# One full-size product in place of the turn and the spread in a kernel's scale chain

## The chip, the core and the metric

The kernel runs on one core of one Trainium2 chip. The core has five engines that work through queues of their own and wait for one another by semaphores: TensorE (PE in the profile, its weight loads PEld), VectorE (DVE), ScalarE (ACT), GpSimd (POOL) and SyncE (SP, which here only issues transfers). The metric is the device time of one execution in microseconds (us); lower is better.

## What is computed

Three stages follow one another, all of them in single precision at the interface: attention with a window of 128 and a distance bias on 4 x 8 heads of 576 positions; a mixture of eight experts over the 2304 tokens that come out, whose weights are normalised by eight rounds over rows and columns; and a feed-forward layer of width 2048 with a leaky maximum.

```python
def _attn_ref(q, k, v):                     # q, k, v: 4 x 8 x 576 x 64
    scores = scale * np.matmul(q, k.transpose(0, 1, 3, 2))
    mask = (rel >= 0) & (rel < 128)
    scores = np.where(mask, scores + bias[None], -1000000000.0)
    attn = np.exp(scores - np.max(scores, axis=-1, keepdims=True))
    attn = attn / (np.sum(attn, axis=-1, keepdims=True) + 1e-09)
    return np.matmul(attn, v)

def _moe_ref(x, w_gate, w1, w2):            # x: 2304 x 512, eight experts of 512 x 1024 x 512
    P = np.exp(x @ w_gate - (x @ w_gate).max())
    for _ in range(8):
        P /= P.sum(1, keepdims=True) + 1e-09
        P /= P.sum(0, keepdims=True) + 1e-09
        P *= N / E
    for e in range(E):
        out += P[:, e:e + 1] * (np.maximum(x @ w1[e], 0.0) @ w2[e])
    return out

def _moe2_ref(x, w_in, w_out):              # 512 x 2048 x 512
    h = x @ w_in
    return np.maximum(0.01 * h, h) @ w_out
```

## The kernel before

**Products.** Every large product is made of float16 matmuls. An operand is split into a high and a low float16 part (`split`), three of the four part products are kept, and a 2 x 2 block product is made with seven products in place of eight (`PRODUCTS`). For float16 to be exact enough, each operand is first multiplied by a power of two that brings its largest entry to a fixed place; the power is taken out again when the result is scaled. The float16 matmuls have 128 rows and 128 columns of weights and mostly 256 columns of moving data; they stand on lines 774 (first layer, results `s` and `sq`) and 891 (second layer, result `t`).

**The scale chain.** `scale_jobs` works out such a power for one operand. It is called 51 times: five times for the attention output of a token group (`Inputs`, phase 0), once for the gate weights, forty times for a chunk of weights (`Weights`, twice for each of the 20 chunks, with `squares=True`) and five times for the input of the last layer (`Inputs`, phase 1). It returns jobs, one a tick, with `None` for ticks that are left out:

- `one` (L453 to L459): VectorE reduces the per-partition values `mx` to one column `m` and keeps the exponent bits of it, `e`.
- `two` (L461 to L478): the column is turned into a row: a matmul with `e`, read as bfloat16, as one column of weights and the bfloat16 identity as 128 columns of moving data gives `mt`, one row of 128. VectorE reduces that row to one number `k` and makes the power and its reciprocal of it, `b`, all on one partition.
- `three` (L480 to L483): the two numbers are spread to all partitions: a matmul with a row of ones, `onesb`, as weights of one row and `b` as two columns of moving data gives `st`, 128 x 2. VectorE copies it to `sr`, from which `scaled` (L625), `turned`, `weigh` and `back` read.

Both results lie in a PSUM bank that `small_psum` gives out: after the attention stage from the same pair of banks that the results `t0` of the second layer use in turn; during it from the one bank `s1`.

**The order.** The work is put into queues (`side`, `inputs`, `gating`, `fill`) from which `tick` takes a job after each step of seven matmul groups or so. The tile framework then orders each engine's instructions by a timeline that it works out itself (`schedule_with_timeline_sim=True`), so that a change of one job can move others, in the attention stage above all, where PE, DVE and ACT have much to choose from. PE, DVE, ACT and POOL take their instructions strictly in the order that results.

**The stages in the trace**, in us from the start: attention, the first weight chunk and the token groups up to about 212; the rounds of the gate beside products up to about 300; the experts up to about 1470; the change from the experts to the last layer, where the inputs are turned, scaled and split again, up to about 1620; the rest of the last layer up to 1904.

Of the kernel before, what the change touches and what calls it, by code (L numbers as in the profile page):

```python
# [8 lines left out]
F32 = mybir.dt.float32  # L9
F16 = mybir.dt.float16  # L10
BF16 = mybir.dt.bfloat16
I32 = mybir.dt.int32
U32 = mybir.dt.uint32
AF = mybir.ActivationFunctionType
ALU = mybir.AluOpType
# [16 lines left out]
def attn_moe_kernel(  # L32
# [12 lines left out]
    nc = tc.nc  # L45
    P = 128
# [23 lines left out]
    const = ctx.enter_context(tc.tile_pool(name="const", bufs=1))  # L70
# [5 lines left out]
    small = ctx.enter_context(tc.tile_pool(name="small", bufs=2))  # L76
# [5 lines left out]
    identb = const.tile([P, P], BF16, name="identb")  # L82
# [3 lines left out]
    ones = const.tile([P, P], F32, name="ones")  # L86
    nc.vector.memset(ones, 1.0)
    shift = const.tile([P, 1], F32, name="shift")
    nc.vector.memset(shift, float(-(896 << 23)))
    onesb = const.tile([1, P], BF16, name="onesb")  # L90
    nc.vector.memset(onesb, 1.0)
    wg = const.tile([P, KT, E], F32, name="wg")
    qscale = const.tile([P, NP], F32, name="qscale")
    Pm = const.tile([P, NTILE, E], F32, name="Pm")
# [74 lines left out]
    def small_psum(shape, name):  # L169
        if "ps_bx" in pools:  # L170
            return pools["ps_bx"].tile(shape, F32, tag="s0", name=name)
        return ps_a.tile(shape, F32, tag="s1", name=name)
# [26 lines left out]
    st = {}  # L199
# [167 lines left out]
    def gate_weights():  # L367
        nc.vector.tensor_reduce(out=gmx, in_=wg, axis=AX.XY, op=ALU.max, apply_absolute_value=True)
        for job in scale_jobs(gmx, 1, srg):
            if job is not None:  # L370
                job()
        nc.vector.tensor_scalar_mul(wg, wg, srg[:, 0:1])
        nc.vector.tensor_copy(wgs[:, :, 0:E], wg)
        nc.vector.tensor_tensor(out=wgs[:, :, E:2 * E], in0=wg, in1=wgs[:, :, 0:E], op=ALU.subtract)
        nc.scalar.activation(out=wgn, in_=wgs[:, 0:KT // 2], func=AF.Copy, scale=-1.0)
# [72 lines left out]
    def scale_jobs(mx, n, sr, squares=False):  # L448


        d = {}

        def one():  # L453
            m = small.tile([P, 1], F32, tag="m", name="m")
            nc.vector.tensor_reduce(out=m, in_=mx[:, 0:n], axis=AX.X, op=ALU.add if squares else ALU.max)
            e = small.tile([P, 1], I32, tag="e", name="e")
            nc.vector.tensor_scalar(out=e, in0=m.bitcast(I32), scalar1=0x7F800000, scalar2=None, op0=ALU.bitwise_and)

            d["mb"] = e.bitcast(BF16)[:, 1:2]  # L459

        def two():  # L461
            mt = small_psum([1, P], "mt")
            nc.tensor.matmul(mt, d["mb"], identb, start=True, stop=True)  # L463
            k = small.tile([1, 1], F32, tag="k", name="k")
            nc.vector.tensor_reduce(out=k, in_=mt, axis=AX.X, op=ALU.max)
            if squares:
                kb = k.bitcast(I32)
                nc.vector.tensor_scalar(out=kb, in0=kb, scalar1=24, scalar2=23,
                                        op0=ALU.logical_shift_right, op1=ALU.logical_shift_left)
                nc.vector.tensor_scalar(out=kb, in0=kb, scalar1=float(64 << 23), scalar2=None, op0=ALU.add)  # L470
            nc.vector.tensor_scalar_max(k, k, 2.0**-28)
            top = TOP + 1 if squares else TOP
            b = small.tile([1, 2], I32, tag="b", name="b")
            nc.vector.tensor_scalar(out=b[:, 0:1], in0=k.bitcast(I32), scalar1=-1.0,
                                    scalar2=float((254 + top) << 23), op0=ALU.mult, op1=ALU.add)
            nc.vector.tensor_scalar(out=b[:, 1:2], in0=k.bitcast(I32), scalar1=1.0,
                                    scalar2=float(-(top << 23)), op0=ALU.mult, op1=ALU.add)
            d["sb"] = b.bitcast(BF16)[:, 1::2]  # L478

        def three():  # L480
            st = small_psum([P, 2], "st")
            nc.tensor.matmul(st, onesb, d["sb"], start=True, stop=True)
            nc.vector.tensor_copy(sr, st)  # L483

        return [one, None, None, two, None, None, three, None]

    def split(hi, lo, src):
        nc.scalar.activation(out=hi, in_=src, func=AF.Copy)  # L488
# [11 lines left out]
    class Inputs:  # L500
# [10 lines left out]
        def scale(self):  # L511

            t0, n = self.t0, self.n
            if self.phase == 0:
                lo = max(t0 - 1, 0)
                return scale_jobs(vmx[:, lo:t0 + 2 * n], t0 + 2 * n - lo, self.sr) + [self.weigh]
            return [lambda k=k: self.largest(k) for k in range(2 * n)] + scale_jobs(self.mx, 2 * n, self.sr) + [self.weigh]
# [569 lines left out]
    for n, u in enumerate(units + [None]):  # L1087
        a, b = [], b_steps(*prev)
        if u == LAST:
            held_back = b[7:]  # L1090
            b = b[:7]
        if u is None:
            b = held_back[:3] + [f for two in zip(b, held_back[3:] + [None] * 3) for f in two if f is not None]
# [9 lines left out]
        if prev[1] == ends[prev[0]] and prev[0] + 1 < NC:  # L1103
            k0 = len(b) - 7
            b = [[f] + ([lambda j=k - k0: W[1][prev[0] + 1].at(j)] if k >= k0 else []) for k, f in enumerate(b)]
        else:
            b = [[f] for f in b]
# [70 lines left out]
```

## Time and profile before

| | |
|---|---|
| time, median of 3 runs | 1906.19 us (1905.77 to 1906.43) |
| the profiled execution: span, first to last instruction | 1904.2 us |
| PE busy | 1840.7 us, 97% of the span |
| ACT, POOL, DVE busy | 72%, 70%, 69% |
| the chain of work that ended last | PE 35%, of it L891 17%, L774 17% (its results `s` 10% and `sq` 7%); ACT 2%, POOL 2%, DVE 1% |

The span is that of one execution under the profiler; the runs have another time, 2.0 us more at the median, so a forecast made in the span is carried over by adding this. Busy time says how much of the span an engine had something in flight. For PE a matmul's own duration (some 270 ns for a large one) is longer than the distance at which the next can start (109 ns), so what a matmul costs is read as the distance between the starts of its neighbours, not as its duration.

### The profile page before, as it was taken

The page shows a single profiled execution, that of the slowest core. Times are in us where ns is not written, and L with a number is a line of the kernel's source. Part 1 is how long each engine was busy: PE and PEld are TensorE (multiplying, and loading weights), DVE is VectorE, ACT ScalarE, POOL GpSimd, SP SyncE. Part 2 cuts the span into 40 slices and gives each one's busy share as a digit, 9 for nine tenths or more (in the row PEclk, how much of TensorE's full clock was granted, in tenths as well). Part 3 has the DMA queues.
Part 4 walks back from the last instruction along what each step waited for, and adds up shares of the span by engine and source line. Part 5 has one row for each costly group of instructions (what it writes and reads, how often), then busy time and mean ns, then how long its engine had stood idle before and what let it go on. Part 6 is the DMA issues. An engine that isn't in the chain of part 4 may idle for free. (4 is left out here: it accounts for less than half of the span.)

```text
span 1904.2 us, 44974 instructions
## 1 busy us (share of the span) xinstructions
PE 1840.7 (97%) x17593; PEld 1602.9 (84%) x17593; DVE 1318.6 (69%) x3621; ACT 1362.9 (72%) x3123; POOL 1335.4 (70%) x1168
## 2 busy tenths in 40 slices
PE   6899889999999999999999999999999998999999
PEld 4677778988888888888888888888989876889888
DVE  5566566677676776767676776666666786677877
ACT  7988768776776767677676757666666769776764
POOL 4854667877878787786878776676866776666753
PEclk8999999999999999999999999999999999999999
DMA  7532002211120212112020210100001010101002
GB/s 227 169 100 83 2 23 73 63 45 56 40 84 22 75 32 76 57 40 63 34 84 24 76 48 29 46 24 23 23 24 46 1 38 9 45 2 45 2 26 76
DMA packets 61094, 97.80 MB, mean 51 GB/s; under 512 B 4561, under 2 KB 27601, under 8 KB 60881
## 3 DMA queue, kind: packets, MB, share of 16 engines
q1 hardware_dynamic: 60880, 94.93, 15.7%
q8 instruction: 137, 2.24, 0.5%
q14 instruction: 77, 0.62, 0.1%
HBM read 81.81 MB, written 13.11 MB: 50 GB/s over the span
## 5 line engine op out<-in xcount | busy, mean ns | idle before, releaser
L891 PE MATMUL t<-w,h 128*128 128x256 f16 x7560 | 972.3, 273 | 21.0 <-ACT acc L898 7.9
L774 PEld LDWEIGHTS <-w 128*128 128x128 f16 x8400 | 757.0, 98 | 99.1 <-issue 16.6
L891 PEld LDWEIGHTS <-h 128*128 128x128 f16 x7560 | 731.7, 98 | 117.7 <-issue 28.4
L774 PE MATMUL s<-xp,w 128*128 128x256 f16 (+1 forms) x4872 | 614.3, 262 | 9.5 <-ACT q L798 3.9
L904 DVE SCALAR_TENSOR_TENSOR acc<-t,pu,acc 128x256 f32<-128x256 f32 x866 | 408.2, 478 | 185.8 <-PE t L891 138.0
L847 POOL TENSOR_TENSOR h<-s,h 128x1024 f16<-128x1024 f32 x180 | 384.0, 2133 | 116.4 <-ACT h L844 77.4
L774 PE MATMUL sq<-xp,w 128*128 128x256 f16 (+1 forms) x3528 | 442.4, 262 | 1.7 <-DVE s L803 1.5
L902 POOL TENSOR_TENSOR acc<-acc,part 128x256 f32<-128x256 f32 x322 | 234.0, 729 | 267.6 <-ACT part L901 240.9
L489 POOL TENSOR_TENSOR w<-raw,w 128x512 f16<-128x512 f32 x240 | 277.6, 1169 | 39.5 <-ACT w L488 39.4
L803 DVE SCALAR_TENSOR_TENSOR h<-sq,h 128x512 f16<-128x512 f32 (+1 forms) x352 | 192.4, 551 | 69.5 <-ACT h L828 36.7
L901 ACT ACTIVATE part<-t,pu 128x256 f32<-128x256 f32 x322 | 151.2, 469 | 103.6 <-PE t L891 97.4
L844 ACT ACTIVATE h<-s 128x1024 f16<-128x1024 f32 x180 | 189.7, 1054 | 46.4 <-DVE s L803 45.6
L790 DVE SCALAR_TENSOR_TENSOR sq<-sq,q 128x256 f32<-128x256 f32 x352 | 150.2, 427 | 86.0 <-PE sq L774 74.0
L786 ACT ACTIVATE q<-s 128x256 f32<-128x256 f32 x364 | 138.0, 381 | 96.4 <-PE s L774 66.3
L488 ACT ACTIVATE w<-raw 128x512 f16<-128x512 f32 x240 | 147.1, 629 | 6.8 <-PE s L774 2.8
L803 DVE SCALAR_TENSOR_TENSOR s<-sq,s 128x256 f32<-128x256 f32 x352 | 145.9, 415 | 2.4
L803 DVE SCALAR_TENSOR_TENSOR s<-sq,q 128x256 f32<-128x256 f32 x352 | 132.5, 414 | 14.6 <-ACT q L798 12.3
L790 DVE SCALAR_TENSOR_TENSOR sq<-s,q 128x256 f32<-128x256 f32 x176 | 75.7, 430 | 93.0 <-ACT q L786 84.1
L822 ACT ACTIVATE h<-sq 128x512 f16<-128x512 f32 x176 | 104.5, 594 | 41.0 <-DVE sq L790 18.7
L622 ACT ACTIVATE junk<-raw 128x512 bf16<-128x512 f32 x160 | 100.3, 627 | 30.0 <-DMA raw<-in_moe_w_dram 28.5
L828 ACT ACTIVATE h<-sq 128x256 f16<-128x256 f32 x176 | 67.2, 382 | 68.6 <-DVE sq L790 59.1
L625 ACT ACTIVATE raw<-raw,sr 128x512 f32<-128x512 f32 x160 | 102.5, 717 | 0.8 <-DVE sr L483 0.6
(152 smaller groups left out, 1716.9 us busy)
## 6 DMA issues: line engine op xcount, KB each, us to landing
raw<-in_moe_w_dram SPq DMA_DIRECT2D x32, 768.0 KB, 4.8
k_t<-in_k_dram SPq DMA_DIRECT2D x16, 512.0 KB, 4.0
raw<-in_moe_w_dram SPq DMA_DIRECT2D x32, 256.0 KB, 4.4
raw<-in_moe_w_in_dram SPq DMA_DIRECT2D x16, 512.0 KB, 3.8
raw<-in_moe_w_out_dram SPq DMA_DIRECT2D x16, 512.0 KB, 3.5
q_t<-in_q_dram SPq DMA_DIRECT2D x18, 256.0 KB, 3.7
v_t<-in_v_dram SPq DMA_DIRECT2D x18, 256.0 KB, 2.7
acc<-in_v_dram SPq DMA_DIRECT2D x18, 256.0 KB, 6.8
```

Source lines behind the costliest of these rows:

```text
L488: nc.scalar.activation(out=hi, in_=src, func=AF.Copy)
L489: return nc.gpsimd.tensor_tensor(out=lo, in0=src, in1=hi, op=ALU.subtract)
L774: nc.tensor.matmul(d[b][:, f, :], t[:, wp, kk, ft * P:(ft + 1) * P], XP[p][:, o, kk, xp, :], start=(i == 0 and f == 0 and j in FIRST), sto ...
L786: nc.scalar.activation(out=q[:, k], in_=ps, func=AF.Copy, scale=CS)
L790: nc.vector.scalar_tensor_tensor(out=block(k), in0=ps, scalar=CS, in1=q[:, k], op0=ALU.mult, op1=ALU.add)
L803: nc.vector.scalar_tensor_tensor(out=out, in0=in0, scalar=sc, in1=in1, op0=op0, op1=op)
L844: nc.scalar.activation(out=h[:, 3:7, 0, :], in_=d["s"], func=AF.Copy)
L847: nc.gpsimd.tensor_tensor(out=h[:, 3:7, 1, :], in0=d["s"], in1=h[:, 3:7, 0, :], op=ALU.subtract)
L891: nc.tensor.matmul(ps, h[:, o, hp, f, tt * P:(tt + 1) * P], w[:, wp, ft, :], start=(i == 0 and j in FIRST), stop=(i == 5), skip_group_chec ...
L901: nc.scalar.activation(out=part, in_=ps, func=AF.Copy, scale=s)
L902: nc.gpsimd.tensor_tensor(out=dst, in0=dst, in1=part, op=ALU.add)
L904: nc.vector.scalar_tensor_tensor(out=dst, in0=ps, scalar=s, in1=dst, op0=ALU.mult, op1=ALU.add)
```

## The change

The exponent column `e` is no longer turned. VectorE multiplies the bfloat16 identity by it, one number for each partition, which makes a 128 x 128 diagonal matrix `dg`, in a buffer of its own. One matmul of a 128 x 128 matrix of bfloat16 ones with `dg` as 128 columns of moving data then gives a 128 x 128 result whose every row holds all 128 exponents. The matrix of ones is a view of the existing single-precision `ones`, the upper two bytes of each number, so it is read with a step of two elements. VectorE reduces the row to `k` on all 128 partitions at once and does the same arithmetic there, with `sr` as its output. The job `three`, its matmul, its PSUM tile and its copy are gone; a `None` stands in its place, so that the lists stay as long as they were.

```diff
-    onesb = const.tile([1, P], BF16, name="onesb")
-    nc.vector.memset(onesb, 1.0)
+    onesb = ones.bitcast(BF16)[:, 1::2]
...
-            d["mb"] = e.bitcast(BF16)[:, 1:2]
+            dg = d["dg"] = small.tile([P, P], BF16, tag="dg", bufs=1, name="dg")
+            nc.vector.tensor_scalar(out=dg, in0=identb, scalar1=e.bitcast(F32), scalar2=None, op0=ALU.mult)
 
         def two():
-            mt = small_psum([1, P], "mt")
-            nc.tensor.matmul(mt, d["mb"], identb, start=True, stop=True)
-            k = small.tile([1, 1], F32, tag="k", name="k")
+            mt = small_psum([P, P], "mt")
+            nc.tensor.matmul(mt, onesb, d["dg"], start=True, stop=True)
+            k = small.tile([P, 1], F32, tag="k", name="k")
             nc.vector.tensor_reduce(out=k, in_=mt, axis=AX.X, op=ALU.max)
...
-            b = small.tile([1, 2], I32, tag="b", name="b")
+            b = sr.bitcast(I32)
...
-            d["sb"] = b.bitcast(BF16)[:, 1::2]
-
-        def three():
-            st = small_psum([P, 2], "st")
-            nc.tensor.matmul(st, onesb, d["sb"], start=True, stop=True)
-            nc.vector.tensor_copy(sr, st)
-
-        return [one, None, None, two, None, None, three, None]
+        return [one, None, None, two, None, None, None, None]
```

Up to L478 the line numbers of the two kernels differ by one at most; further down the changed kernel's are six lower (L768 is the old L774, L784 the old L790, L797 the old L803, L885 the old L891, L898 the old L904, L630 the old L636; in the attention stage L249, L313, L329 and L346 are the old L250, L314, L330 and L347).

PE, in the middle of the experts' stage, at a chain for a chunk of weights, before. `w` and `h` are weights of the large products, `s` and `t` results of the first and the second layer:

```order
L774 LDWEIGHTS w_6198
L774 MATMUL s_7371<-xp_2838,w_6198 128x256
L463 LDWEIGHTS e
L463 MATMUL mt<-identb,e 1x128
L891 LDWEIGHTS h
L891 MATMUL t_7331<-w_6542,h 128x256
```

and, at another chain of that stage, the spread, which stands some 90 rows behind the turn:

```order
L774 LDWEIGHTS w_3151
L774 MATMUL sq<-xp_120,w_3151 128x256
L482 LDWEIGHTS onesb
L482 MATMUL st<-b,onesb 128x2
L891 LDWEIGHTS h
L891 MATMUL t_4300<-w_3983,h 128x256
```

The first of these places now:

```order
L768 LDWEIGHTS w_6168
L768 MATMUL s_7337<-xp_2820,w_6168 128x256
L463 LDWEIGHTS ones
L463 MATMUL mt<-dg,ones 128x128
L885 LDWEIGHTS h
L885 MATMUL t_7297<-w_6512,h 128x256
```

The small matmul stands at the same place between large ones and has become as large in rows and columns of weights as they are; the second small matmul has no successor.

DVE at the same chain as the first piece, from the reduction to the first read of `mt`, before:

```order
L455 TENSOR_REDUCE m<-mxw 128x1
L457 TENSOR_SCALAR e<-m 128x1
L790 SCALAR_TENSOR_TENSOR sq<-sq,q 128x256
L803 SCALAR_TENSOR_TENSOR h<-sq,h 128x256
L803 SCALAR_TENSOR_TENSOR s<-sq,q 128x256
L465 TENSOR_REDUCE k<-mt 1x1
```

and now:

```order
L454 TENSOR_REDUCE m<-mxw 128x1
L797 SCALAR_TENSOR_TENSOR h<-sq,h 128x2x256
L456 TENSOR_SCALAR e<-m 128x1
L459 TENSOR_SCALAR dg<-identb,e 128x128
L784 SCALAR_TENSOR_TENSOR sq<-sq,q 128x256
L465 TENSOR_REDUCE k<-mt 128x1
```

The diagonal comes right behind `e`, and one step of the large products stands between it and the read of `mt`, where three stood between `e` and that read.

PE in the attention stage, from the third chain on, before (`pt`, `s`, `o` and `rt` are attention's own products):

```order
L314 MATMUL rt<-ident,sm 64x128 x4
L463 LDWEIGHTS e
L463 MATMUL mt<-identb,e 1x128
L314 MATMUL rt<-ident,sm 64x128 x4
L250 MATMUL s<-k_t,qs 128x256 x4
L347 MATMUL o<-pb,v_t 64x128 x8
L330 MATMUL pt<-ident,e 128x128 x3
L482 LDWEIGHTS onesb
L482 MATMUL st<-b,onesb 128x2
```

and now, between the same products:

```order
L313 MATMUL rt<-ident,sm 64x128 x8
L249 MATMUL s<-k_t,qs 128x256 x4
L346 MATMUL o<-pb,v_t 64x128 x8
L329 MATMUL pt<-ident,e 128x128 x8
L249 MATMUL s<-k_t,qs 128x256 x4
L463 LDWEIGHTS ones
L463 MATMUL mt<-dg,ones 128x128
L329 MATMUL pt<-ident,e 128x128 x4
L768 LDWEIGHTS w_442
L768 MATMUL s_856<-xp_116,w_442 128x256
```

Here the order of the products around the chains has changed as well: the first large product of the experts' stage starts among attention's products where it came behind the last chain of weights of the first chunk.

## Rows read from the trace of the kernel before

**Rows 1.** Page, part 1: busy time, share of the span, instructions.

```profile
PE 1840.7 (97%) x17593; PEld 1602.9 (84%) x17593; DVE 1318.6 (69%) x3621; ACT 1362.9 (72%) x3123; POOL 1335.4 (70%) x1168
```

**Rows 2.** Busy time by stretch: attention, experts, change to the last layer.

```profile
core 0: us, PE busy (x) PEld busy (x) DVE busy (x) ACT busy (x) POOL busy (x), PEclk, DMA share, GB/s
0.00:212.00 212.00, 182.39 (x1833) 138.21 (x1834) 116.60 (x495) 179.11 (x541) 116.36 (x144) 0.97 0.42 130
...
300.00:1470.00 1170.00, 1163.41 (x11102) 1032.26 (x11100) 818.10 (x2098) 818.20 (x1765) 883.18 (x742) 1.00 0.15 47
1470.00:1620.00 150.00, 136.56 (x1227) 115.47 (x1226) 111.00 (x318) 118.88 (x261) 107.92 (x87) 0.99 0.05 15
```

**Rows 3.** Same view of the turn (L463) alone: PE and PEld busy.

```profile
0.00:212.00 212.00, 1.95 (x9) 0.71 (x9) 0.97 0.42 130
...
1470.00:1620.00 150.00, 1.95 (x9) 0.71 (x9) 0.99 0.05 15
```

**Rows 4.** Timeline of PE around a spread: start us, us, engine, line, what.

```profile
309.20 0.82 PE L774 MATMUL sq<-xp,w 128*128 128x256 f16 x6
309.96 0.17 PE L482 MATMUL st<-b,onesb 1*128 1x2 bf16 x1
310.06 0.61 PE L891 MATMUL t<-w,h 128*128 128x256 f16 x4
```

**Rows 5.** Timeline of PE around a turn.

```profile
493.32 1.25 PE L774 MATMUL s<-xp,w 128*128 128x256 f16 x10
494.51 0.22 PE L463 MATMUL mt<-identb,e 128*1 128x128 bf16 x1
494.66 0.83 PE L891 MATMUL t<-w,h 128*128 128x256 f16 x6
```

**Rows 6.** Timeline of PE at full-size matmuls of 128 moving columns, two places.

```profile
135.17 0.83 PE L774 MATMUL s<-xp,w 128*128 128x256 f16 x6
135.83 0.39 PE L318 MATMUL rt<-turned,sel 112*128 112x128 bf16 x4
...
363.96 0.83 PE L774 MATMUL sq<-xp,w 128*128 128x128 f16 x12
364.63 0.49 PE L891 MATMUL t<-w,h 128*128 128x256 f16 x3
```

**Rows 7.** One line's instructions (L304): ns min/median/max, first and last start, form.

```profile
L304 PEld LDWEIGHTS <-pieces x12: 128/131/133, 85.5 to 195.8; 128*112 128x112 bf16 x12
```

**Rows 8.** DVE groups: busy us, mean ns | idle before.

```profile
L457 DVE TENSOR_SCALAR e<-m 128x1 int32<-128x1 int32 x51 | 7.3, 148 | 0.9
L471 DVE TENSOR_SCALAR k<-k 1x1 f32<-1x1 f32 x51 | 7.0, 137 | 0.9
L483 DVE COPY sr<-st 128x2 f32<-128x2 f32 x40 | 6.1, 154 | 3.6 <-PE st L482 3.4
```

**Rows 9.** L714's instructions, then timelines of POOL, DVE and PE at two.

```profile
L714 DVE TENSOR_SCALAR raw<-raw x32: 408/1498/2329, 278.8 to 1139.5; 128x512 int32<-128x512 int32 x32
...
451.17 2.13 POOL L847 TENSOR_TENSOR h<-s,h 128x1024 f16<-128x1024 f32 x1 [0.48 <-ACT h L844]
...
451.99 1.60 DVE L714 TENSOR_SCALAR raw<-raw 128x512 int32<-128x512 int32 x1
...
389.32 1.85 DVE L714 TENSOR_SCALAR raw<-raw 128x512 int32<-128x512 int32 x1
...
392.34 0.38 PE L891 MATMUL t<-w,h 128*128 128x256 f16 x2 [0.50 <-ACT part L901]
```

**Rows 10.** Timelines of DVE and POOL ahead of the turn of rows 5.

```profile
492.80 0.15 DVE L457 TENSOR_SCALAR e<-m 128x1 int32<-128x1 int32 x1
...
491.49 2.14 POOL L847 TENSOR_TENSOR h<-s,h 128x1024 f16<-128x1024 f32 x1
```

**Rows 11.** PE's waits in attention: total us, times, longest; then the chain, 1500:1530.

```profile
PE s L250 <- POOL qs L209: 5.2, 1, 5.2
...
1514.16 2.09 POOL h L847
```

## The prediction

> **What bounds the kernel now.** I read the busy times first: PE has work in flight for 97% of the span, the others for some 70% [rows 1]. A share over a whole span hides stages, so the busy times by stretch come next. In the experts' stage PE is busy for 1163.41 of 1170 us at a granted clock of 1.00, while POOL, the next, is busy for 883 [rows 2]: there nothing but PE sets the time, and 6.6 us is all that PE's waits cost. In attention PE is busy for 182 of 212 us and ACT for 179; in the change to the last layer PE for 137 of 150 [rows 2]. In those two stages the bound passes from engine to engine, and a saving on PE comes through only in part.
>
> Because PE is full, the question is what one chain costs PE, and busy time does not tell that. The timeline does, by the distances between starts. A large matmul with 256 moving columns starts 0.11 us after the one in front of it: six of them take 135.17 to 135.83 [rows 6].
>
> **What the change removes.** *The spread.* Six large matmuls start at 309.20, so a seventh would start at 309.86; with the spread between them the next large one starts at 310.06 [rows 4]. The spread takes 0.20 us of PE, though it has two moving columns. *The turn.* Ten large ones start at 493.32, the next would come at 494.42 and comes at 494.66 [rows 5]: 0.24 us. Together 0.44 us a chain. The small matmul does not start at the place where the next large one would (309.86, 494.42) but 0.10 and 0.09 us later, and what follows it comes 0.10 and 0.15 us later again. Nothing is waited for in these rows. So most of the price is for going from a full-size matmul to one with a single row or column of weights, and back.
>
> **What it adds on PE.** One matmul of 128 rows and 128 columns of weights with 128 moving columns. Is the price for the shape or for the change from float16 to bfloat16? The rows answer: bfloat16 matmuls with 112 rows of weights start on time behind a float16 one (135.83, six times 0.11 after 135.17) [rows 6], so the data type costs nothing, nor do a few missing rows. And twelve full-size matmuls with 128 moving columns, each with its own weights, take 363.96 to 364.63, 0.056 us each [rows 6]. I take 0.056 us. The bounds are 0.056 and 0.24, the old price of the turn. One thing lies between: the ones are read with a step of two. The nearest row is L304, also bfloat16 read with such a step: its 112 columns load in 131 ns [rows 7]. If that load could not hide behind the large matmul in front of it (0.11 us), the new product would cost up to about 0.11. PE's net gain is 0.44 - 0.056 = 0.384 us a chain.
>
> The Trainium skill speaks against the 0.056: its page "TensorE: Matmul & The Clock Gate", section "Back-to-back issue gap", gives about 81 ns for a matmul of 128 columns in a stream where each has its own weight load, against 56 for matmuls alone. The twelve matmuls of [rows 6] do have their own loads and stand at 56, so here the row disagrees and the row decides; with 81 ns the sum below would be 0.8 us smaller.
>
> **How much of it counts.** There are 51 chains (x51) [rows 8], 9 of them in attention and 9 in the change to the last layer [rows 3]. The other 33 lie where PE is full or nearly so (28 of them in the experts' stretch). There the gain counts in full: 33 x 0.384 = 12.7 us. The 18 could give 18 x 0.384 = 6.9 us; in their stages PE is busy for 86 and 91% [rows 2], but the chain that ended last runs through POOL there for stretches (L847 at 1514.16) [rows 11], and ACT is nearly as full as PE in attention. Ends 0 and 6.9; I take half, 3.5 us.
>
> **What it adds elsewhere.** *DVE.* The copy to `sr` goes (154 ns), the diagonal comes; the small arithmetic stays the same in time, since one column on one partition takes 137 ns and on 128 partitions 148 [rows 8]. The diagonal is an elementwise instruction on SBUF of 128 elements a partition: above the 148 ns of one element and below the 408 ns that L714 needs for 512 when it is not held up [rows 8, 9]. On DVE that would be about even, and DVE is 70% busy. But L714 has a median of 1498 ns: at 451.99 it starts while POOL is inside an instruction that ends at 453.30, and it ends at 453.59, 0.29 us behind it; alone it takes 0.41 [rows 9]. An elementwise instruction of this kind, SBUF to SBUF with one tensor in, is thus held until POOL's current instruction is over, and the diagonal is of this kind. Before, no chain had such an instruction that mattered: reductions, columns and PSUM copies are short. POOL is busy for 75% of the experts' stage with instructions of up to 2.1 us, so a diagonal may be held for up to 2.1 us; queued behind it on DVE are the evictions of the large products, and PE waits for those once their banks are full.
>
> What does that cost PE? From below nothing: the held instruction has slack. `e` ends at 492.95, POOL's instruction at 493.63, and the turn starts at 494.51 [rows 5, 10], so a diagonal that ends 0.3 us behind POOL would be in time by 0.6 us. From above 0.22: 30 of the 32 L714 lie in the stretch from 300 to 1470, most of them held as the median says, and PE's whole idle time there is 6.6 us [rows 2, 9]; 6.6 / 30 = 0.22. The worst single place is 389.32, held for 1.85 us, with PE idle for 0.50 us soon after [rows 9]. I take 0.05 us for each of the 51, nearer to the free end, since the diagonal works on a quarter of the elements and there is room in the place just read: 2.6 us. Bounds 0 and 11.
>
> *Waits and banks.* PE's product now waits for one DVE instruction more, and the two attempts at a PSUM bank become one, so DVE's copy no longer holds a bank that the second layer's results need. `sr` is ready earlier, but its readers stand at the same ticks. I count nothing for these in the experts' stage, where 6.6 us is all that could be won. *Order.* The scheduler has arranged attention anew. What that brings cannot be read from the trace; the largest wait of PE there is 5.2 us, at the start [rows 11], and the 30 us that PE is idle there are the room in both directions. I count 0, with 4 us either way in the range.
>
> **Sum.** 1904.2 - 12.7 - 3.5 + 2.6 = 1890.6 us of span; the median of the runs is 2.0 us above the profiled span, so **1892.6 us**, 0.7% faster.
>
> **The rivals.**
>
> *The price stays with the single product.* If going to any lone small product costs 0.24 whatever its shape, only the spread's 0.20 us is saved: 33 x 0.20 = 6.6, half of 18 x 0.20 = 1.8, less 2.6: 1904.2 - 5.8 + 2.0 = 1900.4. Against it: the bfloat16 matmuls of [rows 6] enter without a gap. 6%.
>
> *All of it comes through.* 51 x 0.384 = 19.6, no cost on DVE, and some of the waits in attention go with the second bank: 1904.2 - 19.6 - 1 + 2.0 = 1885.6. For it: PE's busy share is high in those stages as well. Against it: POOL and ACT on the chain there. 8%.
>
> *The gain goes to a new order in attention.* The first large product now starts among attention's products. If the in-order queues wait there for one operand more, twice the longest wait seen (10.4 us) is lost: 1892.6 + 10.4 = 1903.0, no change within 0.2%. 6%.
>
> *Slower: the diagonal stops PE.* Mechanism: DVE is held by POOL at each diagonal, the evictions behind it are late, and PE stops at a full bank or at the product itself. With the worst place's 0.50 us [rows 9] at all 51: 25.5 us lost against 16.2 gained, 1904.2 + 9.3 + 2.0 = 1915.5. It decides from 16.2 / 51 = 0.32 us a chain. For it: POOL is busy for 75%. Against it: most held L714 leave PE's stretch of 1170 us nearly without idle time. 5%.
>
> The Trainium skill has the rule behind this rival: "SBUF — State Buffer", section "Who interferes with whom", says that VectorE instructions in a two-port mode and GpSimd exclude each other for a whole instruction, and counts `tensor_scalar` among those that can be in such a mode. By that rule the diagonal is held as L714 is; the rows at 451.17 and 451.99 agree.
>
> **How the numbers follow.** The forecast has 75%, the rivals 6, 8, 6 and 5. Its own range: above, only the 33 chains count, the load of the ones is not hidden (33 x 0.05 = 1.7 less), the diagonals cost 0.08 us each and attention loses 2: about 1901; below, everything counts and attention gains 2: about 1884. This takes in the first two rivals and leaves out the last two with a part of the forecast's tails. A measurement of this kernel can tell about 0.2% (3.8 us) from no change: the forecast and the first two rivals are faster, the third is the same, the fourth slower; with a little of the forecast's tail given to both, 88, 7 and 5%.
>
> **What would show it.** In the changed trace the large matmul behind L463 should start 0.056 us later than it would without it, where it was 0.24, and the neighbours should show no gap in front; PE's busy time in the experts' stage should fall by 11 us with its idle time much as before. The diagonal's duration should be 0.2 to 0.4 us when POOL is idle and longer, ending close behind POOL's instruction, when it is not. Wrong would be: a gap of 0.1 us in front of the new product; PE waits for `dg` or for evictions behind it that add up to more than 5 us; or an attention stage whose end has moved by more than 4 us.

## The result, and the profile after

| | before | after |
|---|---|---|
| time, median of 4 runs each | 1906.31 us (1905.77 to 1906.59) | 1926.69 us (1922.14 to 1929.98) |
| ratio, 95% interval | | 1.0109 (1.0091 to 1.0126) |
| span of the profiled execution | 1904.2 us | 1920.1 us |

The forecast was 1892.6 us with a range of 1884 to 1901. The kernel became 20.4 us slower: 34 us from the forecast, and on the other side.

Page of the changed kernel, part 1, and its busy times by stretch (columns as in [rows 2]):

```profile
PE 1832.1 (95%) x17542; PEld 1606.9 (84%) x17542; DVE 1352.3 (70%) x3620; ACT 1354.5 (71%) x3123; POOL 1331.0 (69%) x1168
```

```profile
0.00:212.00 212.00, 185.03 (x1805) 140.71 (x1806) 118.58 (x494) 178.54 (x540) 114.98 (x144) 0.94 0.41 130
...
300.00:1470.00 1170.00, 1144.76 (x10973) 1024.60 (x10971) 834.45 (x2085) 808.74 (x1764) 871.16 (x736) 1.00 0.15 47
1470.00:1620.00 150.00, 136.03 (x1266) 117.95 (x1263) 117.51 (x322) 112.67 (x253) 106.96 (x88) 1.00 0.06 22
```

PE is busy for less than before (1832.1 us after 1840.7), but in the experts' stage it now idles for 25.2 of 1170 us where it was 6.6 [rows 2]. The new product does what was said of it. PE's timeline in the changed kernel:

```profile
652.30 0.49 PE L768 MATMUL s<-xp,w 128*128 128x256 f16 x3
652.63 0.22 PE L463 MATMUL mt<-dg,ones 128*128 128x128 bf16 x1
652.69 0.60 PE L768 MATMUL s<-xp,w 128*128 128x256 f16 x4
```

Three large matmuls from 652.30, the product on time at 652.63, the next large one 0.06 us later: no gap on either side, against 0.24 [rows 5]. So the loss lies elsewhere. PE's waits between 300 and 1470 us (total us, times, longest), first of the changed kernel, then of before:

```profile
PE t L885 <- DVE acc L898: 9.5, 12, 1.6
PE t L885 <- ACT part L895: 7.0, 10, 1.1
PE s L768 <- ACT q L780: 3.4, 4, 1.2
PE s L768 <- ACT q L792: 2.5, 7, 0.6
PE mt L463 <- DVE dg L459: 0.8, 2, 0.5
```

```profile
PE t L891 <- ACT part L901: 2.2, 3, 1.5
PE t L891 <- DVE acc L904: 2.2, 1, 2.2
PE s L774 <- ACT q L798: 1.5, 7, 0.3
```

PE hardly waits for `dg`. It waits for the evictions of its banks, the accumulation on DVE (L898) and the copies on ACT (L895, L780). Two places show two different reasons. DVE and PE at 500 us:

```profile
500.61 0.82 DVE L459 TENSOR_SCALAR dg<-identb,e 128x128 bf16<-128x128 bf16 x1
501.35 0.42 DVE L784 SCALAR_TENSOR_TENSOR sq<-sq,q 128x256 f32<-128x256 f32 x1
...
501.48 0.22 PE L463 MATMUL mt<-dg,ones 128*128 128x128 bf16 x1 [0.52 <-DVE dg L459]
```

and at 304 us:

```profile
304.78 0.43 DVE L697 TENSOR_SCALAR raw<-raw 128x512 int32<-128x512 int32 x1 [2.68 <-DMA raw<-in_moe_w_in_dram]
305.12 0.48 DVE L898 SCALAR_TENSOR_TENSOR acc<-t,pu,acc 128x256 f32<-128x256 f32 x1
...
305.65 0.81 PE L885 MATMUL t<-w,h 128*128 128x256 f16 x6 [0.91 <-DVE acc L898]
```

In the first, `dg` is held (0.82 us; its median is 254 ns). In the second nothing of the chain is near: DVE's queue stands for 2.68 us at the first instruction of a cast job (one of 32 that make a piece of the last layer's weights ready on DVE, ACT and POOL; L697, the old L703), whose transfer has not landed; the eviction L898 stands behind it, and PE waits for that. Between 300 and 1160 us DVE waits nine times for a cast's transfer in the changed kernel, 8.2 us in all, and not once in the kernel before: the scheduler, given another chain, has put the casts at other places of DVE's queue. So there are two theories: **the hold** (the added DVE instruction) and **the arrangement** (the new order of instructions that the diff does not touch).

### The profile page after: what moved, and what is told of

Read it like the earlier page. It is cut to its first block, busy times and chain, and to the rows that moved or that the text cites. A ratio compares the mean times of both kernels' runs of the same rounds, so it can differ in the third digit from the quotient of the medians.

```text
span 1920.1 us, 44857 instructions
## 1 busy us (share of the span) xinstructions
PE 1832.1 (95%) x17542; PEld 1606.9 (84%) x17542; DVE 1352.3 (70%) x3620; ACT 1354.5 (71%) x3123; POOL 1331.0 (69%) x1168
## 5 line engine op out<-in xcount | busy, mean ns | idle before, releaser
L885 PE MATMUL t<-w,h 128*128 128x256 f16 x7560 | 981.3, 273 | 27.5 <-DVE acc L898 11.8
L768 PEld LDWEIGHTS <-w 128*128 128x128 f16 x8400 | 761.5, 98 | 111.8 <-issue 32.7
L885 PEld LDWEIGHTS <-h 128*128 128x128 f16 x7560 | 732.5, 98 | 125.5 <-issue 38.2
L768 PE MATMUL s<-xp,w 128*128 128x256 f16 (+1 forms) x4872 | 608.8, 262 | 15.0 <-ACT q L780 6.6
L898 DVE SCALAR_TENSOR_TENSOR acc<-t,pu,acc 128x256 f32<-128x256 f32 x866 | 406.7, 478 | 194.1 <-PE t L885 156.4
L768 PE MATMUL sq<-xp,w 128*128 128x256 f16 (+1 forms) x3528 | 446.2, 262 | 5.9 <-DVE s L797 3.3
L797 DVE SCALAR_TENSOR_TENSOR h<-sq,h 128x512 f16<-128x512 f32 (+1 forms) x352 | 193.5, 552 | 73.6 <-ACT h L816 37.0
L895 ACT ACTIVATE part<-t,pu 128x256 f32<-128x256 f32 x322 | 152.1, 472 | 125.3 <-PE t L885 112.8
L838 ACT ACTIVATE h<-s 128x1024 f16<-128x1024 f32 x180 | 189.6, 1053 | 60.1 <-DVE s L797 58.9
L784 DVE SCALAR_TENSOR_TENSOR sq<-sq,q 128x256 f32<-128x256 f32 x352 | 149.7, 427 | 68.5 <-PE sq L768 54.1
L780 ACT ACTIVATE q<-s 128x256 f32<-128x256 f32 x364 | 136.8, 379 | 80.7 <-PE s L768 52.1
L797 DVE SCALAR_TENSOR_TENSOR s<-sq,s 128x256 f32<-128x256 f32 x352 | 146.0, 415 | 2.2
L797 DVE SCALAR_TENSOR_TENSOR s<-sq,q 128x256 f32<-128x256 f32 x352 | 131.9, 415 | 8.9 <-ACT q L792 5.5
L784 DVE SCALAR_TENSOR_TENSOR sq<-s,q 128x256 f32<-128x256 f32 x176 | 75.5, 429 | 86.5 <-ACT q L780 80.4
```

The costliest lines, as they stand in the source:

```text
L768: nc.tensor.matmul(d[b][:, f, :], t[:, wp, kk, ft * P:(ft + 1) * P], XP[p][:, o, kk, xp, :], start=(i == 0 and f == 0 and j in FIRST), sto ...
L780: nc.scalar.activation(out=q[:, k], in_=ps, func=AF.Copy, scale=CS)
L784: nc.vector.scalar_tensor_tensor(out=block(k), in0=ps, scalar=CS, in1=q[:, k], op0=ALU.mult, op1=ALU.add)
L797: nc.vector.scalar_tensor_tensor(out=out, in0=in0, scalar=sc, in1=in1, op0=op0, op1=op)
L838: nc.scalar.activation(out=h[:, 3:7, 0, :], in_=d["s"], func=AF.Copy)
L885: nc.tensor.matmul(ps, h[:, o, hp, f, tt * P:(tt + 1) * P], w[:, wp, ft, :], start=(i == 0 and j in FIRST), stop=(i == 5), skip_group_chec ...
```

## The experiments

To tell them apart, the chain and the order must be changed one at a time. In the runs "held to an order", the other kernel's instructions are listed engine by engine, and each instruction is tied behind its neighbour in that list by an edge that fixes the order of issue and waits for nothing:

```diff
+for a, b in zip(seq, seq[1:]):            # seq: one engine's instructions in the wanted order
+    tc.add_manual_dep(ins[b], ins[a].name, order_only, reason="order")
```

| run | chain | `dg` on | order of the rest | us, median | ratio to before (95%) |
|---|---|---|---|---|---|
| before | old | - | its own ("old") | 1906 | 1 |
| after | new | DVE | its own ("new") | 1926.7 | 1.0109 (1.0091 to 1.0126) |
| e1 | new | DVE | old | 1909.8 | 1.0018 (1.0006 to 1.0029) |
| e2 | old | - | new to 78% | 1967.8 | 1.0315 (1.0288 to 1.0342) |
| e3 | new | DVE | old in the experts alone | 1920.0 | 1.0065 (1.0039 to 1.0090) |
| e4 | old, turn one job earlier | - | free | 1921.2 | 1.0074 (1.0052 to 1.0095) |
| e5 | new | ACT | old | 1908.4 | 1.0010 (1.0000 to 1.0020) |
| e6 | old, and a spare `dg` | DVE | old | 1918.4 | 1.0063 (1.0042 to 1.0083) |
| e7 | new | ACT | new | 1930.0 | 1.0119 (1.0101 to 1.0136) |
| e8 | new | ACT | free | 1916.6 | 1.0054 (1.0035 to 1.0073) |
| **e9** | new without `dg` | - | old | **1894.7** | 0.9940 (0.9927 to 0.9952) |
| e10 | new without `dg` | - | new | 1920.5 | 1.0080 (1.0064 to 1.0096) |
| e11 | new | DVE | old to 300 us | 1926.6 | 1.0114 (1.0085 to 1.0142) |
| e12 | new | DVE | old from 1470 us | 1920.5 | 1.0077 (1.0063 to 1.0091) |
| e13 | as e9, short casts | - | old | 1882.0 | 0.9866 (0.9852 to 0.9881) |
| e14 | as e9, short casts | - | new | 1903.2 | 0.9978 (0.9969 to 0.9988) |
| e15 | as e9 | - | old on PE alone | 1940.6 | 1.0172 (1.0153 to 1.0191) |
| e16 | as e9 | - | free | 1915.7 | 1.0047 (1.0030 to 1.0063) |
| e17 | as e14, short loads | - | new | 1897.2 | 0.9958 (0.9944 to 0.9972) |
| e18 | as e13, short loads | - | old | 1882.7 | 0.9881 (0.9866 to 0.9896) |

The kernel before, run beside them, had medians of 1905.7 to 1908.7 us.

**e1, the new chain in the old order.** 

> The changed chain, with every other instruction of every engine held in the order that it has in the kernel before; dg stands right behind e on VectorE, the spread and its copy are gone. Theory A (the new arrangement of the instructions costs the time, the chain itself saves): the sum of the forecast holds, 1892.6 us, between 1886 and 1898, and TensorE idles about 7 us between 300 and 1470 us. Theory B (the added dg itself, on VectorE's queue and held by GpSimd, stops TensorE): 1915 us or more, with TensorE idle over 20 us in the same stretch.

17 us come back, and 17 are still missing against the forecast: neither theory has it all. Here `dg` can be watched with everything else as before. DVE, POOL and PE of e1 (L471 is `dg`, L895 and L939 are before's L847 and L891):

```profile
500.00 1.41 DVE L471 TENSOR_SCALAR dg<-identb,e 128x128 bf16<-128x128 bf16 x1
...
499.24 2.12 POOL L895 TENSOR_TENSOR h<-s,h 128x1024 f16<-128x1024 f32 x1
...
502.58 0.81 PE L939 MATMUL t<-w,h 128*128 128x256 f16 x6 [0.90 <-ACT part L949]
```

`dg` ends at 501.41, 0.05 us behind POOL. The next eviction on DVE is late, ACT waits for that one (3.19 us, for L838), its copy of PE's bank comes behind it, and PE stops for 0.90 us. `dg` is held at the second chain of all ten chunks between 300 and 1100 us, for 0.48 to 1.41 us. And one hold in attention was long:

```profile
78.91 5.45 DVE L471 TENSOR_SCALAR dg<-identb,e 128x128 bf16<-128x128 bf16 x1
...
78.61 1.17 POOL L537 TENSOR_TENSOR w<-raw,w 128x512 f16<-128x512 f32 x1
79.72 0.21 POOL L303 TENSOR_TENSOR pieces<-pieces 128x8 f32<-128x8 f32 x1
79.88 2.15 POOL L537 TENSOR_TENSOR xp<-sx,xp 128x1024 f16<-128x1024 f32 x1
81.97 0.22 POOL L303 TENSOR_TENSOR pieces<-pieces 128x8 f32<-128x8 f32 x1
82.13 1.18 POOL L537 TENSOR_TENSOR xp<-acc,xp 128x512 f16<-128x512 f32 x1
83.24 1.06 POOL L215 TENSOR_TENSOR qs<-q_t,qscale 128x512 f32<-128x512 f32 x1
```

It outlasts six POOL instructions that follow each other without a pause.

**e2, the old chain in the new order; e3, the old order in the experts' stage; e4, the old chain with its turn one job earlier.** The last is this edit and no other:

```diff
-        return [one, None, None, two, None, None, three, None]
+        return [one, None, two, None, None, None, three, None]
```

> The chain of the kernel before, with the other instructions of the attention and experts' stages (the first 78% of the program, to about 1540 us) held in the order of the changed kernel; the chain's own instructions stand where the scheduler finds room. Theory A: slower than the changed kernel, since it pays for the new arrangement (about 30 us) and for the two one-sided products: 1926 to 1945 us, with TensorE idle at least 20 us between 300 and 1470 us. Theory B: the time of the kernel before, 1900 to 1912 us.

> The changed chain, held to the order of before only in the experts' stage (12% to 73% of the program, some 300 to 1470 us). Theory A: the 18.6 us by which TensorE idles more in that stretch come back and the rest of the loss stays, 1908 us, between 1902 and 1914. Theory B: as the changed kernel, 1920 to 1932 us.

> The kernel before with the turn's job one place earlier in the list that spreads the chain over the groups (third instead of fourth); the work is the same, the scheduler arranges all engines anew. It shows what a new arrangement alone can do. Theory A: the time leaves that of before by more than 4 us, either way (1895 to 1902 or 1910 to 1930 us). Theory B: within 4 us of 1906 us.

e4 settles that an arrangement alone can do it: the same work, 15 us slower. e3 gives back only 6.7 of the 18.6 us that theory A put there and stands at the lower end of theory B's range; the hold is still in it. e2 came out far above either theory, and its trace shows why it does not count as a price of the arrangement: the two small products, left to the scheduler in a fixed surrounding, made PE wait themselves (waits from 300 to 1160 us, then from 1160 to 1480).

```profile
PE st L527 <- DVE b L521: 13.2, 14, 1.4
...
PE mt L508 <- DVE e L502: 6.1, 2, 3.4
```

**e5 to e8, where `dg` is written, and a spare one.** e5, e7 and e8:

```diff
-            nc.vector.tensor_scalar(out=dg, in0=identb, scalar1=e.bitcast(F32), scalar2=None, op0=ALU.mult)
+            nc.scalar.activation(out=dg, in_=identb, func=AF.Copy, scale=e.bitcast(F32))
```

e6 adds the first of these lines to the kernel before; nobody reads its `dg`.

> As the run with the changed chain in the old order, but dg is written by ScalarE (a copy scaled by e) and not by VectorE; all else is held in the order of the kernel before. Theory hold (in that run dg stood on VectorE until GpSimd's instruction in flight had ended, up to 5.4 us, and the evictions behind it came late): the chain's saving now shows, 1887 to 1898 us, with TensorE idle less than 9 us between 300 and 1160 us. Rival (another part of the changed chain is at fault, its full-size product's PSUM bank or the reduction over 128 partitions): 1904 us or more, as with dg on VectorE (1909.8).

> The kernel before in its own order, with a dg written on VectorE behind e that nobody reads; the chain's products and the rest are those of before (the row of ones is taken from the tile of ones, to make room for dg). Theory hold: the spare instruction alone makes it 1916 to 1930 us, since the changed chain in this order lay 17 us above the forecast. Rival: 1904 to 1910 us, as before plus nothing.

> The changed kernel in its own order, with dg written by ScalarE. What is left against the run with dg on ScalarE in the old order is the price of the arrangement by itself. Theory hold and order, each with a share: 1908 to 1922 us (the waits that start at dg in the changed kernel's trace sum to 8 to 11 us, so 1926.7 less about 10). Theory hold alone: 1900 us or less. Theory order alone: 1924 us or more.

> dg on ScalarE and nothing held: the scheduler arranges all engines anew. By the theory that an arrangement costs 0 to 30 us by chance: anything from 1890 to 1925 us, most likely 1900 to 1920 us. By the theory that only the hold matters: 1887 to 1898 us.

e6 is the clean one: a `dg` that takes part in nothing makes the old kernel 12 us slower, so the added instruction alone has a price of this size here. Where it is paid can be read by comparing the starts of the same second-layer matmuls (7560 in each trace) with those of the kernel before: 4.9 us are lost up to 235 us, where one `dg` is held for 5.46 us, and 5.9 us from 300 to 1140 us, where the casts are; from 1180 to 1470 us, without casts, nothing is lost, though two `dg` are held there for 1.3 us each. So a hold costs time in some stretches and none in others.

e5 missed its number; by the number its rival holds, but e9 below, which has the same product and reduction without `dg`, rules that rival out. On ACT `dg` is never held (L474: 385 to 447 ns in all 51). The reason is in PE's waits, here of attention:

```profile
PE mt L480 <- ACT dg L474: 9.6, 3, 3.5
```

In all 17.7 us in nine places. Its place on ACT was left to the scheduler, and it is a bad one there: the queue reaches `dg` late, or stands at it until `e` is written. e7 and e8 move `dg` out of the hold as well and stay at 1930 and 1917 us; by its expectation e7 speaks for the order alone. But there too PE waits for `dg` on ACT, 13.2 us in e7 and 3.1 in e8, so these three say little on the price of the hold.

**e9 and e10, no `dg` at all.** The product can be had without a diagonal: `e` itself, one column repeated over 128 by a stride of zero, as weights, and the identity as moving operand.

```diff
-            nc.tensor.matmul(mt, onesb, d["dg"], start=True, stop=True)
+            nc.tensor.matmul(mt, e.bitcast(BF16)[:, 1:2].to_broadcast([P, P]), identb, start=True, stop=True)
```

> The changed chain without dg: the full-size product takes e itself, one column spread over 128 as weights by a stride of zero, and the identity as moving operand, which gives the same values on all partitions; spread and copy are gone, all else is held in the order of the kernel before. If the forecast's price of the two small products holds (16.2 us in 51 chains) and only dg and the arrangement spoilt it: 1890 us, between 1885 and 1896, with TensorE idle under 8 us between 300 and 1160 us. If the products are worth only the 8.6 us by which the changed chain with dg lay below the old chain with a spare dg: 1896 to 1900 us. If something else of the changed chain costs time: 1903 us or more.

> The same chain without dg, all else held in the order of the changed kernel. The price of the arrangement by itself: if it adds to the chain's saving, 17 to 22 us above the run without dg in the old order, about 1907 to 1915 us. If the arrangement costs only by what it does with dg: within 5 us of that run.

e9 lies 2 us from the forecast, within the forecast's range, and beats both kernels. That it comes so near is partly luck: the forecast holds 2.6 us for a diagonal that e9 does not have, and the saving itself fell short by 4.8 us. Its weights load in 96 to 98 ns, as those of the large products do (98):

```profile
L484 PEld LDWEIGHTS <-e x51: 96/98/98, 14.6 to 1758.3; 128*128 128x128 bf16 x51
```

From 300 to 1160 us PE idles for 8.5 us, a little more than the 8 expected. Its stretch from 300 to 1470 us, and PE's waits there up to 1160 us (L836, L953 and L963 are before's L774, L891 and L901):

```profile
300.00:1470.00 1170.00, 1161.48 (x11172) 1041.88 (x11170) 823.67 (x2088) 825.51 (x1783) 887.60 (x745) 1.00 0.15 47
```

```profile
PE t L953 <- ACT part L963: 4.4, 6, 1.4
PE s L836 <- ACT q L860: 2.9, 13, 0.3
```

e10 is the same program in the other order, and is 25.8 us slower, more than either expectation. Its waits in the same stretch have the pattern of the changed kernel, without any `dg`:

```profile
PE t L953 <- DVE acc L966: 8.7, 11, 1.6
PE t L953 <- ACT part L963: 5.8, 7, 1.1
PE s L836 <- ACT q L848: 2.8, 4, 1.0
```

The two traces lie 24.9 us apart. By the starts of the same matmuls, 9.7 us of this are lost before 300 us, 12.2 from 300 to 1140, beside the casts, and 3.0 behind. In the first of these parts PE's granted clock differs as well: 0.93 of full speed up to 212 us and 0.96 in the gate in e10, against 0.98 and 1.00 in e9 (the changed kernel: 0.94 and 0.96, before: 0.97 and 1.00). How much of the 9.7 us goes through the clock is not shown. From 300 to 1470 us it is 1.00 in both, so the larger part has nothing to do with it.

**e11 and e12, the old order in the first or in the last stages.**

> The changed kernel, held to the order of before only in the first 12% of the program (attention and gate, to about 300 us). If the 17 us of the arrangement are shared over the stages: 1919 us, between 1913 and 1923, with the 5.1 us wait of the gate's cp product for its column sums gone. If the loss sits in the experts alone: 1924 us or more.

> The changed kernel, held to the order of before only in the last 27% of the program (from about 1470 us). If the loss is shared over the stages: about 6 us less than the changed kernel, 1917 to 1923 us. If it sits in attention and experts alone: 1925 us or more.

By its expectation e11 puts the loss in the experts alone, while e12 says that it is shared. With e3, the parts give back 0, 6.7 and 6.2 of the 17 us; the shares do not add up. In the changed kernel's gate PE stands once for 5.1 us at the product of the column sums:

```profile
PE cp L431 <- DVE c L427: 5.1, 1, 5.1
```

e11 has no such wait and yet the changed kernel's time, so this wait, the longest of the gate, is not shown to cost anything at the end; e11's runs scatter widely (1920.9 to 1936.6).

**e13 to e18, what in the arrangement costs it.** In e13 and e14 the three DVE instructions of each cast job work on one column (the second layer's last weights are then not cast, so that part of the result is left out); in e17 and e18 the cast's load also moves an eighth of the columns.

```diff
-            nc.vector.tensor_scalar(out=d["fac"], in0=d["hi"], scalar1=20, ...
+            nc.vector.tensor_scalar(out=d["fac"][:, 0:1], in0=d["hi"][:, 0:1], scalar1=20, ...
...
-            nc.sync.dma_start(flat[:, 0:2 * FC], src)
+            nc.sync.dma_start(flat[:, 0:FC // 4], src[:, 0:FC // 4])
```

> The chain without dg in the old order; in the 32 cast jobs the three VectorE instructions (L703, L709 and L714 of before) work on one column instead of 512 and the scale of the ScalarE step behind the first is 1, so that the second layer's last weights are not cast: that part of the result is left out. All instructions stay where they are. It is the partner of the next run; against the run with whole casts (1894.7): 2 to 6 us less, 1888 to 1893 us.

> The same short casts and chain without dg, in the order of the changed kernel. Theory casts (in the new order the casts' three VectorE instructions, held by GpSimd and waiting for their DMA, stand close together between the evictions, and that is the 13 us of the experts' stage): the new order then loses under 5 us between 300 and 1160 us against its partner, and in all 10 to 15 us, 1899 to 1907 us. Rival (the order of TensorE's groups or ScalarE's evictions themselves): the loss against the partner stays at 22 us or more, 1912 us or more.

> The chain without dg; TensorE alone is held to the order of before, the scheduler arranges the other engines anew. If the order of TensorE's groups carries the loss: 1893 to 1899 us. If the order on VectorE, ScalarE or GpSimd carries it: 1905 us or more.

> The chain without dg and nothing held: what the simple edit alone would give. By the theory that any new arrangement of this program loses 15 to 26 us against that of before: 1908 to 1921 us. If the order of the changed kernel was an unlucky one: 1890 to 1905 us.

> As the run with short casts in the changed kernel's order, and the load of each cast job moves an eighth of its columns (128 of 1024 words a row); what the casts should give is left out as there. All instructions stay where they are. Theory transfer wait (in the new order VectorE's queue reaches the cast's first instruction before its transfer has landed, 14.7 us in 8 places, and the evictions behind it hold TensorE): the load lands sooner, the wait falls under 5 us, and 1893 to 1898 us are measured. Rival (the places of the evictions and of ScalarE's passes among themselves): 1900 to 1905 us, as with the whole load (1903.2).

> Its partner in the order of before, which has that wait in one place only (3.5 us): within 4 us of the run with short casts and whole loads in that order, 1877 to 1884 us, by either theory. What is left between the two is then the price of the arrangement without casts and without the transfer wait: by the theory 12 to 18 us, by the rival 20 us or more.

e13 missed its range: it is 12.7 us faster than e9, where 2 to 6 were expected. By the starts, nearly all of it is won from 300 to 1140 us, where the casts are, although PE's idle time falls only from 8.5 to 2.2 us there (e9, then e13):

```profile
300.00:1160.00 860.00, 851.48 (x8166) 762.22 (x8164) 618.17 (x1554) 620.21 (x1335) 667.53 (x557) 1.00 0.17 54
...
300.00:1160.00 860.00, 857.76 (x8264) 771.70 (x8263) 580.06 (x1575) 626.77 (x1353) 669.39 (x567) 1.00 0.17 54
```

The rest was hidden. A large matmul is in flight for 273 ns and the next can start after 109, so the first 0.16 us by which a start is late do not show as idle time. Added up from the distances between starts from 300 to 1140 us, large matmuls are late by 14.1 us in e9 and by 3.7 in e13. The 32 casts on DVE, held or not, thus cost some 0.3 to 0.4 us each in e9.

The gap between the two orders is 25.8 us with whole casts (e10 less e9), 21.3 with short ones and 14.6 with short loads too. The theory that the casts' work makes the difference between the orders fell: it carries under 5 us. (e14's 1903.2 us lie in that theory's range only because its partner gained more than expected.) The transfers carry about 7. With short casts DVE still waited for them in the new order (e14, DVE's waits from 300 to 1160 us):

```profile
DVE raw L766 <- DMA raw<-in_moe_w_in_dram: 8.6, 3, 3.1
DVE raw L766 <- DMA raw<-in_moe_w_out_dram: 5.6, 4, 2.2
```

and in e17 hardly any more:

```profile
DVE raw L767 <- DMA raw<-in_moe_w_in_dram: 2.3, 3, 1.4
```

14.6 us of the arrangement's price stay open. By the starts in e17 and e18, whose traces lie 13.2 us apart, 3.6 us are lost before 300 us, 6.5 from there to 1140 and 3.1 later. From 300 us on PE's waits in e17 are all under 2 us, for evictions on ACT and DVE; before that there are longer ones, of 3.9 us in attention and 5.1 us in the gate. Which displaced instruction starts each was not traced. e15 shows that PE's order alone does not bring the old time back: with PE in the old order and the other engines free it is the slowest of this chain, 46 us above e9. That points to how the queues fit each other, but the other engines were not tried one by one. And no free arrangement came near the old one: 1921.2 (e4), 1916.6 (e8), 1915.7 (e16) and 1926.7 us (after). Why the kernel before has a better one is not shown.

## Why the prediction was wrong

Two steps failed: the order, which the sum put at nothing, and the diagonal's 2.6 us. A third, how much of the saving counts, was too large by 5 us.

One way through the runs adds up to the result: before to e9, the chain's products alone, -11.4 us; e9 to e1, `dg` on DVE, +15.2; e1 to after, the arrangement, +16.8; together +20.6, and +20.4 were measured. The other way, e9 to e10 to after, gives the arrangement +25.8 and `dg` +6.2: the two overlap. Both act through late evictions on DVE and ACT, which would explain it; that was not tested.

- **What bounds the kernel.** Right from 1160 to 1470 us. Where the casts are, "6.6 us is all that PE's waits cost" was too low: e13 wins 11 us there by shortening work on DVE, 6.3 of them from PE's idle time.
- **The price of the spread, the turn and the new product.** Right. The new product starts on time and costs 0.056 us (rows at 652.63). The first rival, that the price stays with a lone product, is out, and so is the slower load of the strided ones. One sum beside this term is wrong: with 81 ns for the product the saving would be smaller by 0.8 us on the 33 chains, or 1.1 with half of the 18, and so the forecast time longer, not smaller.
- **How much of it counts.** The term was mis-sized: 16.2 us forecast, 11.4 measured (e9). By the starts of the same second-layer matmuls in the traces, e9 gains nothing on before up to 300 us, 9.6 us from 300 to 1470, where 28 chains in full would be 10.8, and 2.8 later. From 1180 to 1437 us, without casts, 2.2 us are gained on some 6 chains: nearly the full 0.384. From 300 to 1100 us, with casts, 20 chains give 3.4 us where 7.7 were due; there PE's waits for ACT rose from 2.2 and 1.5 us to 4.4 and 2.9. (The 4.0 us between hold two chains and a stretch of 3.4 us in which before was granted the lower clock, 1.2 GHz, and e9 was not; up to 1.7 us of them are the clock's, by luck.) PE at 99% busy does not mean that nothing stands close behind it. The second rival, that all of it comes through, is out.
- **The diagonal on DVE.** This step failed in its size. The mechanism was right, with rows that answer to [rows 9]: the hold, and its end 0.05 us behind POOL. 0.05 us a chain was wrong by a factor of five: 12 us (e6) to 15 us (e1 against e9), above the bound of 11. The bound took the 6.6 us of PE's idle time as all that 30 held casts cost; e13 shows that the casts' work on DVE costs nearly twice that, part of it hidden behind matmuls in flight. And 5.45 us in attention were beyond any hold that had been read. By the starts in e1 and e9, which share the order, 3.9 us are lost up to 235 us; between 300 and 1145 us the ten held `dg` cost 0.8 us each, and the ten that were let in at once still 0.3; from 1145 to 1475 us, without casts, nothing is lost, though four were held. So part of the price is no hold, but DVE's time next to the casts. The Trainium skill ("SBUF — State Buffer", "Who interferes with whom") has the second to issue blocked until the first finishes; at 78.91 the trace of e1 differs, the block lasting over six instructions.
- **The slower rival** (held `dg`, 1915.5 us, 5%) was the right mechanism and deserved more, but it is the smaller part of the result. The third rival named the order, but for attention alone, with 10.4 us.
- **The order.** This step failed. It looked at attention alone ("I count 0, with 4 us either way in the range"), and the experts' stage, three fifths of the span, had no term for it; 17 us (e1 to after) or 26 (e9 to e10) were lost; in the traces of e9 and e10, 9.7 us of it before 300 us and 14.3 from there to 1470. What was said of that stage, that 6.6 us is all that could be won, says nothing of a loss: an order in which the queues fit so well has nearly all to lose.

Of the signs named, "PE waits for evictions that add up to more than 5 us" is what showed the forecast wrong. The other two did not appear: there is no gap in front of the product, and attention's last product `o` starts at 198.5 us where it was 197.6.

## What to carry to other kernels

When a scheduler orders the engines, a small edit changes two things, the work and the order of all the rest, and here the second was larger than the first: hold the old order while you time the edit, and time the old work in another order to see what an arrangement is worth. Idle time left on a full engine says nothing of what can be lost there, and where its instructions overlap it does not even bound what can be won, since short delays hide in the overlap. Before adding an instruction to a queue that another engine can hold, look for a form that needs none: here the weights' stride of zero replaced the whole diagonal, and in the old order that made a kernel 0.6% faster than before.

## What the runs showed of the hardware

- Weights read with a stride of zero over their 128 columns cost nothing extra: L484 of e9 loads in 96 to 98 ns, and the next large matmul starts 0.056 us behind the product in 40 of 51 places.
- A held DVE instruction is not always let in at the next boundary between POOL instructions: at 500.00 in e1 it was, at 78.91 it stood for 5.45 us through six of them, back to back; the spare `dg` of e6 has the same longest time, 5459 ns. Nearly every held `dg` ends 0.05 us behind a POOL instruction.
- The same copy of 128 columns takes some 255 ns on DVE when POOL is idle, and 401 ns (median) on ACT whatever POOL does. The Trainium skill ("SBUF — State Buffer", "Who interferes with whom") says of the ports of SBUF that PE and ACT never wait on anyone; for ACT all 51 rows of e5 agree (385 to 447 ns), for PE no run here tests it.
